# Three weight chunks ahead of the first gathers, and the rows of three experts turned by VectorE

## The chip, the cores and the metric

The kernel runs on one core of one Trainium2 chip. The metric is the device time of one execution in microseconds (us). TensorE does the matrix products, VectorE and ScalarE the element-wise work and the copies out of PSUM, GpSimd issues the gathers, scatters and accumulating DMAs, and SyncE issues the other DMAs.

## What is computed

Eight batches of eight heads go through a linear attention with a decay for each head, and the 4608 rows of 512 that come out go to eight experts. A routing by sorted scores gives each expert 576 rows.

```python
scores = scale * np.matmul(q, k.transpose(0, 1, 3, 2))
ret = scores * Dmat[None, :, :, :]          # gamma ** (i - j), lower triangle
x = np.matmul(ret, v)                        # -> 4608 x 512
...
for idx in order:                            # order = argsort(-(x @ w_gate).flatten())
    tok, e = idx // 8, idx % 8
    if assigned[tok] >= 0 or counts[e] >= 576: continue
    assigned[tok] = e; counts[e] += 1
...
for e in range(8):
    h = np.maximum(x[assigned == e] @ w1[e], 0.0)    # 512 -> 1024
    out[assigned == e] = h @ w2[e]                   # 1024 -> 512
```

## The kernel before

The attention runs over 16 units (a pair of batches by a pair of heads, loop `u`), its loads written ahead on SyncE's queue. Its rows go to a tile `xd` in DRAM. `Route` then finds the experts one after the other, in the order in which they fill up ("first" to "eighth" expert below, `e` = 0 to 7 in the code). For each it has a search in seven rounds (a matmul at L353, a chain of VectorE steps before and after), `members`, and `listing`, which writes the row numbers; what it does for the next experts is mixed into the products of the present one.

Each expert is a first layer `l1` and a second layer `l2`. `l1` works in 16 parts: eight blocks `f` of 128 features by two halves `s` of the tokens (256 and 320). A part is 12 matmuls, since weights and rows are each split into a high and a low half (`w1h`, `w1l`, `xh`, `xl`; three of four products are used). ScalarE writes the part's high half `hb` from PSUM (L1055), VectorE its low half (L1058). The parts' PSUM tiles have the tags `h0` and `h1` (by `s`), two buffers each, and `y` for the features 2 and 5. Parts alternate between the two halves; the first expert alone does the 256-token parts of `f` 0 to 3 first, then the 320-token ones. `l2` works in five groups `t` (four of 128 tokens, one of 64) of eight steps `f`, and each group's result `yt` is copied out (L1109; L1111 and a VectorE addition at L1112 for the last) and scattered by GpSimd (L1069).

A weight matrix comes in four chunks of 512 KB. `dma_pump` has SyncE fetch them into four `raw` buffers (L932) up to the limit `state['most']`; `conv` makes ScalarE write the high half (L946) and the negated low half (L951), to which GpSimd adds the chunk by an accumulating DMA (L952). With `fast`, VectorE makes the low half (L949). The limit is 2 until the first expert's rows are there: SyncE waits for the third gather (L1144), and after that the limit is 4, then open. `conv` is called in `l1` after the parts named in a list (L1063) and in `l2` at four steps.

The rows of an expert are gathered by GpSimd: five gathers of 128 rows (L983), then turned by TensorE (20 transposes at L1015, copied by ScalarE at L1017 and subtracted by VectorE at L1018). From `PIECES` on, 18 gathers of quarter rows (L971; VectorE makes their row numbers `quarter` at L476 to L480), turned by VectorE in blocks of 32 (L999), copied at L1001 and subtracted at L1002. All five blocks of such an expert are then written ahead of its first part.

The order in which all this is written is set by a planner (`Mixer`): it counts time for TensorE (`adv`: 320 or 400 for three matmuls of the first layer, 650 for a step of the second) and for VectorE (`vec`), and writes the next step of the search when its time has come. A gathered piece is due every 1300; the turning begins 6000 after the last piece (9000 after five whole gathers). Each engine then works through its own instructions in the order written. `warm` issues matmuls on constants, whose results nobody reads.

Of the kernel before, what the change touches and what calls it, by code (L numbers as in the profile page):

```python
# [19 lines left out]
NP, HP, NB = 4, 4, 9  # L20
N, DM, E, FF = 4608, 512, 8, 1024
SLACK = 1.0
PIECES = 6

def consts_np():
    h = np.arange(H); g = (1.0 - 2.0 ** (-5.0 - h)).astype(np.float64)
# [502 lines left out]
def attention(tc, nc, P, qk, vk, cst_d, wg_d, rf, xd, Lg, raw):  # L529
# [264 lines left out]
    def fills(u, g):  # L794
        for f, a in fill.get(2*u + g, []): f(*a)

    P['warm'](7)
    qscale(0, (0, 512))
    kscale(0, 0, 8)
    scores(0, 0)  # L800
# [92 lines left out]
def moe(tc, nc, P, R, xd, w1_d, w2_d, out, mix):  # L893
# [3 lines left out]
    ready = lambda k: len(found) > k  # L897
    regs, XG, quarters, parts = {}, {}, {}, {}
    xq = xd.rearrange("n (a c) -> (n a) c", a=4)
    state = dict(dma=0, conv=0, most=2, listing=-1)  # L900
    RAW, W1, W2, XH, XL = {}, {}, {}, {}, {}
    scat, lows = [], []
    spacer, spacer2 = [P['c'].tile([1, 1], F32, name=f"spacer{i}") for i in range(2)]
# [118 lines left out]
    def l1(e, tr):  # L1022

        hb = P['w'].tile([128, 8, 1152], F32R, name="hb", bufs=1)
        order = [(f, s) for f in range(8) for s in range(2)]
        if e == 0:
            order[:8] = [(f, s) for s in range(2) for f in range(4)]
        for i, (f, s) in enumerate(order):
            wh, wl = [w.rearrange("p (f d m) -> p f d m", f=2, d=4)[:, f % 2] for w in W1[e, f // 2]]
            if i == 0 and e >= PIECES:  # L1030
                for _ in tr:
                    pass
            if i == 0 and e:
                next(tr, None)
                next(tr, None)
            elif e == 0 and i in (2, 3):
                next(tr, None)
            elif i == (1 if e else 4):
                for _ in tr:
                    pass  # L1040
            xh, xl = XH[e], XL[e]
            c, n = ((slice(0, 256), 256), (slice(256, 576), 320))[s]

            ps = P['pp'].tile([128, n], F32, name="ph", tag="y" if f in (2, 5) else f"h{s}", bufs=2)
            terms = [(w[:, d], x[:, d, c]) for d in range(4) for w, x in ((wh, xh), (wh, xl), (wl, xh))]
            if e == 0 and f < 2:
                terms = terms[0::3] + terms[2::3] + terms[1::3]
            elif i in (2, 3) and e == 0:
                terms = terms[0::3] + terms[1::3] + terms[2::3]
            for k, (w, x) in enumerate(terms):  # L1050
                T.matmul(ps, w, x, start=(k == 0), stop=(k == 11))  # L1051
                if k % 3 == 2:
                    mix.adv(320 + 80*s, e == 0 and i < 3)
                    gather(e + 1)
            A.activation(hb[:, f, c], ps, AF.Relu)  # L1055
            for a, b in ((0, 256),) if s == 0 else ((0, 256), (256, 320)):
                to = (640 if a == 0 else 64) + 256*s
                V.scalar_tensor_tensor(hb[:, f, to+a:to+b], ps[:, a:b], 0.0, hb[:, f, 256*s+a:256*s+b].bitcast(F32),  # L1058
                                       op0=ALU.max, op1=ALU.subtract)
            mix.vec(340 + 140*s)  # L1060
            if e == 0 and i == 4:
                state['most'] = 8*E
            if i in ((2, 4, 7, 10) if e else (3, 5, 7, 9, 11, 13)):  # L1063
                conv()
        return hb

# [59 lines left out]
    def run():  # L1126
        mix.drain(lambda: 0 in regs)
        dma_pump()
        mix.drain(lambda: ready(0))
        conv(True)  # L1130
        conv()
        gather(0)
        lows.pop(0)()
        mix.step()
        warm(25)
        tr = transposes(0)
        next(tr)
        warm(4)
        next(tr)
        lows.pop(0)()  # L1140
        mix.step()
        warm(2)

        nc.sync.dma_start(spacer2, XG[0][0:1, 2, 0:1])  # L1144
        state['most'] = 4
        dma_pump()
        for e in range(E):
            tr = l2(e, l1(e, tr))
# [73 lines left out]
```

## Time and profile before

| what | value |
|---|---|
| three runs | 620.79, 623.42, 626.26 us; median 623.42 |
| profiled execution | 625.75 us, span 623.6 us |
| TensorE busy | 600.7 us (96%) |
| VectorE, ScalarE, GpSimd busy | 410.6, 271.6, 248.2 us |
| mean granted clock of TensorE | 0.988 of full speed |
| moved by DMA | 133.22 MB |

The span is the time from the first to the last instruction that the profile shows. The first expert's first layer begins near 168 us; the eighth expert ends near 620.

### The profile page before, as it was taken

What the parts mean: (1) busy time and instruction counts of PE and PEld (TensorE: products, weight loads), DVE (VectorE), ACT (ScalarE), POOL (GpSimd) and SP (SyncE); (2) the same over time, 40 slices, a digit from 0 to 9 for tenths busy, and PEclk for the clock granted to TensorE, in tenths of its full rate; (3) what the DMA queues carried; (4) which work ended last, traced back from release to release, by engine and by line L of the source; (5) the groups of instructions that cost most, each with busy time, mean ns of one, the idle gap of its engine ahead of it and who ended that gap; (6) DMA issues with size and microseconds to landing.
All of it is one profiled execution on the core that took longest, in us unless ns stands there. A gap on an engine that the chain in (4) does not pass through costs nothing.

```text
span 623.6 us, 14775 instructions
## 1 busy us (share of the span) xinstructions
PE 600.7 (96%) x5722; PEld 518.1 (83%) x5722; DVE 410.6 (66%) x1488; ACT 271.6 (44%) x465; POOL 248.2 (40%) x295
## 2 busy tenths in 40 slices
PE   7899999998989999999999999999999999999995
PEld 5788888875579779988987897799789889989983
DVE  4556788888868888887885877689478733322200
ACT  2244433333347355461652447155526445554410
POOL 4886665500302172061243242224313877832111
PEclk8899999999989999999999999999999999999998
DMA  9999899854768589787789399659937897994501
GB/s 330 408 369 401 280 370 316 261 140 137 192 180 194 174 221 264 186 207 236 156 224 246 94 229 227 201 111 231 247 114 174 200 245 169 259 249 124 102 35 42
DMA packets 53496, 133.22 MB, mean 214 GB/s; under 512 B 7410, under 2 KB 22642, under 8 KB 53426
## 3 DMA queue, kind: packets, MB, share of 16 engines
q0 software_dynamic: 15376, 51.92, 38.0%
q1 hardware_dynamic: 37906, 80.10, 38.0%
q8 instruction: 45, 0.74, 0.5%
q10 hardware_dynamic: 144, 0.26, 0.1%
q14 instruction: 25, 0.20, 0.1%
HBM read 80.35 MB, written 18.87 MB: 159 GB/s over the span
## 4 chain that ended last, share of the span: by engine, by line
PE 74%; DVE 9%; issue 6%; DMA 6%; POOL 2%; ACT 1%; SPq 1%; POOLq 0%; DVEq 0%
PE ph L1051 28%; PE py L1092 28%; PE sc L603 4%; PE px L647 3%; DMA xg<-xd,idx 2%; PE pS L624 2%; PE px L638 2%; PE pT L679 1%; DMA raw<-in_w 1%; PE r L353 1%; PE pt L1015 1%; DVE am L612 1%; DMA qin<-in_qk 1%; DVE cst L544 1%; DMA nin<-in_vk 1%
## 5 line engine op out<-in xcount | busy, mean ns | idle before, releaser
L1092 PE MATMUL py<-w2h,hb 128*128 128x512 f32 x576 | 187.3, 397 | 0.0
L1051 PE MATMUL ph<-xh,w1h 128*128 128x320 f32 (+1 forms) x512 | 151.7, 302 | 3.2 <-ACT xh L1017 3.2
L1051 PE MATMUL ph<-xh,w1l 128*128 128x320 f32 (+1 forms) x512 | 149.2, 297 | 0.0
L1051 PE MATMUL ph<-xl,w1h 128*128 128x320 f32 (+1 forms) x512 | 149.0, 297 | 0.0
L1092 PE MATMUL py<-w2l,hb 128*128 128x512 f32 (+1 forms) x320 | 125.3, 392 | 0.0
L1092 PEld LDWEIGHTS py<-w2h,hb 128*128 128x128 f32 x576 | 104.5, 188 | 21.7
L1051 PEld LDWEIGHTS ph<-xh,w1h 128*128 128x128 f32 x512 | 96.4, 191 | 4.4 <-ACT xh L1017 3.8
L1055 ACT ACTIVATE hb<-ph 128x256 fp32r<-128x256 f32 (+1 forms) x128 | 51.9, 408 | 105.1 <-PE ph L1051 96.3
L1051 PEld LDWEIGHTS ph<-xl,w1h 128*128 128x128 f32 x512 | 96.4, 191 | 0.3
L1051 PEld LDWEIGHTS ph<-xh,w1l 128*128 128x128 f32 x512 | 96.4, 191 | 0.0
L1058 DVE SCALAR_TENSOR_TENSOR hb<-ph,hb 128x256 fp32r<-128x256 f32 (+1 forms) x192 | 58.0, 352 | 46.2 <-ACT hb L1055 39.4
L1069 POOL DMA_INDIRECT out_y<-yt,idx x40 | 40.5, 1013 | 105.7 <-ACT yt L1109 70.5
L1092 PEld LDWEIGHTS py<-w2l,hb 128*128 128x128 f32 (+1 forms) x320 | 56.7, 177 | 12.9
L952 POOL DMA_DIRECT2D w2l<-raw x32 | 29.4, 919 | 87.2 <-ACT w2l L951 48.2
L612 DVE TENSOR_TENSOR am<-sc,cst 128x1024 f32<-128x1024 f32 x32 | 39.1, 1223 | 33.1 <-PE sc L603 33.0
L588 POOL TENSOR_TENSOR qin<-qin,cst 128x512 f32<-128x512 f32 (+1 forms) x48 | 48.3, 1034 | 31.2 <-DMA qin<-in_qk 27.3
L1109 ACT ACTIVATE yt<-py 128x512 f32<-128x512 f32 x32 | 19.2, 599 | 93.6 <-PE py L1092 70.0
L983 POOL DMA_INDIRECT xg<-xd,idx x30 | 30.2, 1008 | 71.9 <-DMA raw<-in_w 37.0
L627 ACT ACTIVATE st<-pS,cst 128x128 f32<-128x128 f32 x64 | 23.5, 368 | 79.9 <-PE pS L624 79.9
L952 POOL DMA_DIRECT2D w1l<-raw x31 | 29.0, 959 | 49.0 <-ACT w1l L951 32.5
L603 PE MATMUL sc<-qin,kin 64*128 64x128 f32 x512 | 38.8, 293 | 3.7 <-DVE am L612 1.9
L971 POOL DMA_INDIRECT xg<-xd,quarter x36 | 35.6, 989 | 12.8 <-issue 9.4
(191 smaller groups left out, 939.0 us busy)
## 6 DMA issues: line engine op xcount, KB each, us to landing
raw<-in_w SPq DMA_DIRECT2D x56, 512.0 KB
w2l<-raw POOLq DMA_DIRECT2D x32, 512.0 KB
w1l<-raw POOLq DMA_DIRECT2D x31, 512.0 KB
qin<-in_qk SPq DMA_DIRECT2D x14, 576.0 KB
kin<-in_qk SPq DMA_DIRECT2D x14, 576.0 KB
vin<-in_vk SPq DMA_DIRECT2D x14, 576.0 KB
nin<-in_vk SPq DMA_DIRECT2D x14, 512.0 KB
xd<-raw SPq DMA_DIRECT2D x36, 128.0 KB
```

The lines of the kernel that those rows point to most:

```text
L588: nc.gpsimd.tensor_tensor(x, x, e[:, None, :n].to_broadcast([128, (b-a)//n, n]), op=ALU.mult)
L603: nc.tensor.matmul(t[:, h, 128*j:128*j+128], blk(k, 4*g+j)[r], blk(q, 4*g+j)[r], start=(j == 0), stop=True, skip_group_check=True)
L612: nc.vector.tensor_tensor(a, SC[u, g].rearrange("p h (j q) -> p h j q", q=128), m1[:, u % HP, :, None, :].to_broadcast([128, 2, 4, 128]), ...
L627: nc.scalar.activation(s, p, AF.Copy, scale=ss[:, u % HP, c:c+1])
L952: add = lambda: nc.gpsimd.dma_start(lo, raw, accum_op=ALU.add)
L971: nc.gpsimd.indirect_dma_start(out=t[:, k, :], out_offset=None, in_=xq[:, :], in_offset=bass.IndirectOffsetOnAxis(ap=quarters[e][:, v:v+1] ...
L983: nc.gpsimd.indirect_dma_start(out=xg[:n, j, :], out_offset=None, in_=xd[:, :], in_offset=bass.IndirectOffsetOnAxis(ap=found[e][:n, j:j+1] ...
L1051: T.matmul(ps, w, x, start=(k == 0), stop=(k == 11))
L1055: A.activation(hb[:, f, c], ps, AF.Relu)
L1058: V.scalar_tensor_tensor(hb[:, f, to+a:to+b], ps[:, a:b], 0.0, hb[:, f, 256*s+a:256*s+b].bitcast(F32), op0=ALU.max, op1=ALU.subtract)
L1069: st = nc.gpsimd.indirect_dma_start(out=out[:, :], out_offset=bass.IndirectOffsetOnAxis(ap=found[e][:n, t:t+1], axis=0), in_=y[:n], in_off ...
L1092: T.matmul(ps[:m], a, w, start=(k == 0), stop=(k == last), skip_group_check=True)
```

## The change

The limit of chunks before the gathers is 3 instead of 2; the third chunk's conversion stands behind the first two blocks' transposes, ahead of the first expert's loop, and is taken out of the loop's list. `PIECES` is 5 instead of 6: the sixth expert joins the seventh and the eighth in having its rows gathered by quarters and turned by VectorE (its weights are then read in the layout `w1n`). For these three, the 256-token parts of `f` 0 to 3 come first, as they do for the first expert, and of their five blocks at most three are written ahead of the first part, one each ahead of the third and the fourth, the rest ahead of the fifth. At the start of the attention 12 matmuls of `warm` instead of 7.

```diff
-PIECES = 6
+PIECES = 5
...
-    P['warm'](7)
+    P['warm'](12)
...
-    state = dict(dma=0, conv=0, most=2, listing=-1)
+    state = dict(dma=0, conv=0, most=3, listing=-1)
...
-        if e == 0:
+        if e == 0 or e >= PIECES:
             order[:8] = [(f, s) for s in range(2) for f in range(4)]
...
-            if i == 0 and e >= PIECES:
-                for _ in tr:
-                    pass
             if i == 0 and e:
+                for _ in range(3 if e >= PIECES else 2):
+                    next(tr, None)
+            elif (e == 0 or e >= PIECES) and i in (2, 3):
                 next(tr, None)
-                next(tr, None)
-            elif e == 0 and i in (2, 3):
-                next(tr, None)
-            elif i == (1 if e else 4):
+            elif i == (4 if e == 0 or e >= PIECES else 1):
                 for _ in tr:
                     pass
...
-            if i in ((2, 4, 7, 10) if e else (3, 5, 7, 9, 11, 13)):
+            if i in ((2, 4, 7, 10) if e else (5, 7, 9, 11, 13)):
                 conv()
...
         next(tr)
         lows.pop(0)()
+        conv()
         mix.step()
```

## Rows read from the trace of the kernel before

**Rows 1.** Busy time by stretches: stretch, then each engine's us, clock, DMA share, GB/s.

```profile
404.10:460.70 56.60, 56.60 (x402) 49.70 (x401) 42.04 (x181) 26.72 (x42) 17.47 (x23) 1.00 0.75 192
460.70:513.90 53.20, 53.20 (x338) 47.71 (x338) 35.92 (x138) 26.88 (x42) 30.90 (x36) 1.00 0.75 181
```

**Rows 2.** Timeline of TensorE: start, us, instruction, idle time before it and its releaser.

```profile
17.51 0.45 PE L624 MATMUL pS<-vin,ks 128*64 128x64 f32 x8 [2.07 <-POOL ks L593]
...
179.00 1.44 PE L1051 MATMUL ph<-xh,w1h 128*128 128x320 f32 x4 [3.02 <-ACT xh L1017]
```

**Rows 3.** Busy time by stretches, behind these two idle times.

```profile
18.60:21.90 3.30, 3.30 (x44) 2.85 (x42) 0.00 (x0) 0.96 (x2) 3.30 (x4) 0.50 1.03 413
...
179.00:182.35 3.35, 3.35 (x12) 3.35 (x13) 0.41 (x1) 0.00 (x0) 0.97 (x1) 0.50 1.00 302
```

**Rows 4.** Timeline of ScalarE around the first expert's first layer.

```profile
169.99 0.38 ACT L1055 ACTIVATE hb<-ph 128x256 fp32r<-128x256 f32 x1 [1.79 <-issue]
...
176.68 1.06 ACT L946 ACTIVATE w1h<-raw 128x1024 fp32r<-128x1024 f32 x1 [0.70 <-DMA raw<-in_w]
...
178.58 0.36 ACT L1017 ACTIVATE xh<-pt 128x256 fp32r<-128x256 f32 x1
```

**Rows 5.** Timeline of SyncE's queue, the first expert's weight chunks.

```profile
157.08 0.89 SPq L932 DMA_DIRECT2D raw<-in_w  x2
...
172.25 13.30 SPq L932 DMA_DIRECT2D raw<-in_w  x5
```

**Rows 6.** Busy time of a stretch of the attention with idle time.

```profile
73.40:78.00 4.60, 3.59 (x73) 3.19 (x73) 4.46 (x8) 1.67 (x5) 2.31 (x3) 1.00 0.53 117
```

**Rows 7.** The same for the stretch behind the second chunk's landing.

```profile
162.50:163.50 1.00, 1.00 (x6) 0.45 (x5) 1.00 (x3) 1.00 (x2) 0.70 (x2) 1.00 0.00 0
```

**Rows 8.** Timeline of TensorE at the start.

```profile
1.48 3.17 PE L1175 MATMUL warm<-full 128*128 128x512 bf16 x7 [1.48 <-DVE full L1161]
6.37 0.83 PE L603 MATMUL sc<-qin,kin 64*128 64x128 f32 x10 [1.72 <-POOL qin L588]
```

**Rows 9.** Timeline of TensorE, first and last of the sixth expert's five runs of transposes.

```profile
431.75 0.51 PE L1015 MATMUL pt<-ident,xg 128*128 128x128 f32 x4
432.09 0.70 PE L1092 MATMUL py<-w2h,hb 128*128 128x512 f32 x2
...
436.12 0.51 PE L1015 MATMUL pt<-ident,xg 64*128 64x64 f32 x4
436.55 0.74 PE L1092 MATMUL py<-w2h,hb 128*128 128x512 f32 x2
```

**Rows 10.** Busy time of VectorE alone while it makes `quarter`.

```profile
477.85:479.38 1.53, 1.35 (x9) 1.00 0.56 102
```

**Rows 11.** Timeline of GpSimd: first gathers of the first, sixth, seventh expert, the seventh's last.

```profile
162.03 1.15 POOL L983 DMA_INDIRECT xg<-xd,idx  x1 [37.01 <-DMA raw<-in_w]
...
422.62 1.07 POOL L983 DMA_INDIRECT xg<-xd,idx  x1 [1.73 <-DVE room L494]
...
479.66 1.07 POOL L971 DMA_INDIRECT xg<-xd,quarter  x1 [2.21 <-DVE eb L504]
...
508.39 0.96 POOL L971 DMA_INDIRECT xg<-xd,quarter  x1 [0.30 <-issue]
```

**Rows 12.** Timeline of VectorE, turning the seventh expert's rows.

```profile
506.70 0.71 DVE L999 STREAM_TRANSPOSE xz<-xg 128x512 f32<-128x512 f32 x1
507.34 0.65 DVE L1002 TENSOR_TENSOR xl<-xz,xh 128x512 fp32r<-128x512 f32 x1
...
513.07 0.45 DVE L999 STREAM_TRANSPOSE xz<-xg 128x256 f32<-128x256 f32 x1 [2.79 <-DMA xg<-xd,quarter]
...
514.64 0.68 DVE L1112 TENSOR_TENSOR yt<-yt,py 64x512 f32<-64x512 f32 x1 [0.22 <-ACT yt L1111]
```

**Rows 13.** The chain that ended last, a piece of a second layer.

```profile
328.63 5.56 PE py L1092 x24
```

**Rows 14.** Busy time of VectorE alone in one round of the search.

```profile
455.88:458.70 2.82, 2.50 (x13) 1.00 0.51 173
```

## The prediction

> **What bounds the kernel now.** I read the busy time by stretches first. In the sixth expert's 53.2 us, as in the fifth's 56.6, TensorE is busy for every microsecond, VectorE for two thirds or more, GpSimd for a third to over a half [rows 1]. So a microsecond is won in three ways only: less work on TensorE, less idle time of it, or a higher granted clock. Then I listed TensorE's idle times. One stands out in the expert stage: 3.02 us in the first expert, ended by ScalarE's copy into `xh` at L1017 [rows 2]. The stretch behind it is granted 0.50, 1.2 in place of 2.4 GHz [rows 3]. ScalarE's own order tells why the copy is late: it stands behind the two conversions of a weight chunk (L946, L951), which begin at 176.68 when the chunk lands, and ends at 178.94 [rows 4]. SyncE issued that chunk at 172.25, as it has to wait for the gathered rows first (L1144); the two chunks before it went out at 157.08 [rows 5].
>
> **First expert: third chunk early, its conversion before the loop.** The transposes of the last block end at 175.98, 3.02 before 179.00 [rows 2]. With the conversions gone, the copy (0.36) [rows 4] follows at once, and the part of 320 tokens begins near 176.5: idle time 0.5 in place of 3.0, a gain of 2.5. That part has 12 matmuls in 3.35 us at 0.50 [rows 3]; at full clock they take half, so 1.65 more, if the clock stays. The stretch around 73.4 to 78, with 1.0 us idle, kept 1.00 [rows 6]; 2.1 us (15.4 to 17.5) and 3.02 us were followed by 0.50 [rows 2, 3]. I count 1.65 in full. Sum: -4.15.
> Where the conversion goes: ScalarE stands idle for 1.79 us up to 169.99 [rows 4], and the conversions need 2.1 (two of 1.06). The first activation of the loop starts some 0.3 later; its bank is wanted again three parts on, so that is nothing. If the chunk were not there by then, ScalarE would wait in front of the copies, as now, and the gain would be gone; but two chunks issued at 157.08 are in at 162.0 [rows 11], and no byte moves from 162.5 to 163.5, ahead of the first gather's rows [rows 7]. 512 KB at 413 GB/s, the rate when the engines are full [rows 3], is 1.3 us. So the third chunk fits between 162 and 163.5 almost whole. I charge 0.2 for its tail; its bounds are 0 and 1.3 (all of it ahead of the gathers), and a fall of the clock on top.
> On GpSimd the accumulating DMA is the next thing behind the five gathers, before as after, only earlier; on SyncE the third issue (0.45) is followed only by the wait at L1144. The chunk for features 768 on is now alone behind that wait. Cost nothing; should it come late, there are ten parts until it is used.
> **The 12 warm-up matmuls.** Five more at the pace of the seven (0.45) are 2.3 us, against 1.72 idle before the first scores [rows 8]: at most 0.5 late, less if the clock is up by then. What follows waits for the loads and GpSimd's scaling until 17.5 [rows 2], whatever TensorE does before it. Taken as 0, bounds -0.5 and +0.5.
> **Sixth expert: TensorE's transposes go.** Five runs of four, each between two `py` matmuls; by start to start the first costs 0.34, the last 0.43, the five 1.63 together [rows 9]. Gain 1.6.
> What replaces it: 18 gathers instead of 5 on GpSimd. They start 1.5 us later (eight small VectorE steps for `quarter`, L476 to L480, 1.53 in all) [rows 10], at 424.1 instead of 422.6, and the run of 18 with the weight and output DMAs among them took 479.66 to 508.39 for the seventh expert [rows 11]: the last starts near 453 to 454 and is in memory 4.7 us later (508.39 to 513.07) [rows 11, 12], at 458.5. The expert's first layer starts at 460.7 - 1.6 = 459.1. The weight accumulations queued among the gathers come some 5 us later, and they are wanted 10 us or more after that: nothing.
> When is it turned? I counted the planner's own figures (a piece each 1300, turning 6000 after the last piece, a step of the second layer 650). For the kernel before they put the seventh expert's first turn at step f=4 of group t=3, ahead of `yt`'s addition, as the trace has it [rows 12]. For the change they put the sixth expert's turns at t=3, f=5 to t=4, f=2, directly behind the search round after f=3, with the next round ahead of the last block.
> VectorE's queue then is, from the end of the second layer (459.1) backwards: the last group 3.7, four steps of 0.70 (24 matmuls in 5.56) [rows 13], so that round's matmul is done at 452.5. A round holds VectorE for 2.8 (455.88 to 458.70) [rows 14]: free at 455.3. Seven turns and subtractions at 0.65 [rows 12] take it to 459.9; the second block's low half, the fifth of them, is ready at 458.6, in time for the first part. The next round, 2.8, to 462.7. Last block 0.45, ScalarE's copy 0.4, its `yt` copy 0.6, VectorE's addition 0.7, and the first part's low half 0.4: 465.2. This is the new wait: with four 256-token parts in a row, the fourth takes the PSUM bank of the first (tag h0, two buffers, the third part uses y). Parts of 256 take 256/320 of 1.7, 1.4, so the fourth is due at 459.1 + 4.2 + a search matmul 0.2 = 463.6. TensorE waits 1.5. In the order before, that bank was wanted three parts later. Whether the clock falls behind 1.5 us lies between the rows (1.0 kept it, 2.1 did not): 0 or up to 1.65, taken as 0.
> **Seventh expert.** The turns put into the search by the planner (1310 a block in place of 610) push its listing from the ninth part of the first layer to the eleventh, 3200 by the same count, or 3.4 us (a part of 1280 takes 1.4): the gathers start that much later against the first layer's start. Before, the last block was there 0.9 before that start (513.07 against 513.9); now it comes 2.5 behind it. From there the same chain, 0.45 + 0.45 + 0.6 + 0.7 + 0.4 = 2.6, gives 5.1, and the bank is due at 4.3: a wait of 0.8. In the old order it would have been 2 or more, since the second part wants all blocks.
> **Eighth expert.** Its rows are there far ahead; the order alone costs nothing.
> **Sum.** -4.15 + 0.2 - 1.6 + 1.5 + 0.8 = -3.25. The profiled execution (625.75, span 623.6) would become 622.5; the median of the three runs, 623.42, becomes 620.2.
>
> **Rivals.** *No new waits.* If VectorE runs as far ahead as it did for the seventh expert before (its third block turned at 506.7, 7 us ahead of need) [rows 12], the waits of 1.5 and 0.8 vanish: -5.55, 617.9. For it: TensorE idles nowhere in the last three experts. Against: there the search was over, while in the fifth expert's stretch, where the sixth's rows are turned, VectorE has 42 of 56.6 us of work [rows 1].
> *The turning comes too late (slower).* Place: end of the sixth expert's second layer. If the seventh's pieces are written later than I count, by three steps of 650, the turns fall into the first layer and stand behind `yt`'s addition: 0.6 + 0.7, then five operations of 0.65 until the second block's low half, 4.6 us of idle TensorE, and 1.65 for the clock. -3.25 - 0.8 + 6.25 = +2.2: 625.6. It decides from those three steps on; my count leaves just this much, and it met the order before. The same at the sixth expert as well would come to 630.
> *The third chunk holds up the first gathers.* In the trace before, the gathers' rows do not move before 163.5 [rows 7], and GpSimd's first gather starts at 162.03, released by that chunk's landing as the trace puts it [rows 11]. If that is no accident, the third chunk's 1.3 us is paid in full, TensorE's warm-up runs out, and the clock may fall: 1.1 to 2.75 worse than the forecast, 621.3 to 623.0; the change then gives little. Here a rule of the Trainium skill speaks against the change: "DMA: Bandwidth & Descriptors", section "SWDGE vs HWDGE vs iDMA", has GpSimd's and SyncE's transfers in different queues of the same engines, served in turn. By that rule gathers beside a chunk get a part of the engines' time instead of waiting behind it, so a cost between nothing and this rival's; no run so far shows a chunk beside the first gathers.
> *It does not do what it says:* the chunk lands after 168.2, and ScalarE waits in front of the loop: no gain of 4.15, 624.3.
>
> **How the numbers follow.** Forecast 0.45, no new waits 0.25, late turning 0.10, held gathers 0.17, no effect 0.03. The range takes the forecast with waits of 0 to 3 in place of 2.3, and the first three rivals: the low end, 616.5, is the first rival less the start's 0.5 and less 0.9, since the three runs of before lie 5.5 us apart; the high end is the second. A measurement of this kernel tells 1% from nothing, 6.2 us: under 617.2 is reached only by the first rival with a little help at the start (0.18), over 629.7 only by late turning twice (0.06).
>
> **What would show it.** After: no idle over 1 us before L1051 in the first expert, clock 1.00 there, conversions of the third chunk in front of the first activation; the first gather at 162.0 to 162.4; no L1015 in the sixth expert; idle time before the fourth first-layer part of the sixth and seventh experts, released by L1058 or L1055. I am wrong if the first gather starts over 1 us later, if the clock falls in the sixth expert, or if `yt`'s addition stands ahead of the seventh's turns.

## The result, and the profile after

| | before | after |
|---|---|---|
| median (22 runs each, side by side) | 622.37 us (619.87 to 626.26) | 628.02 us (622.13 to 632.8) |
| ratio of after to before, 95% interval | | 1.0061 (1.0041 to 1.0080) |
| profiled execution, span | 625.75, 623.6 us | 631.76, 630.0 us |

By the ratio the change makes the kernel slower by 0.6%, 3.8 us; the forecast was 3.2 us faster, and 628.0 lies outside its range. Executions that were slow as a whole (four of after's 22, from 631.60 us up, the profiled one among them) are left out of every ratio and of the medians under "The experiments"; after's median without them is 627.0. The profiled execution of after lies 3.7 us over its own median, so what its trace shows is read stage by stage, and the sizes are taken from the repeated runs.

A table by stage is made from TensorE's timeline: the start of the first matmul of each layer, and the difference to the next one's start. Only these stages differ by more than 0.1 us:

| stage | before | after | difference | forecast |
|---|---|---|---|---|
| attention, up to the first expert's first layer | 168.25 | 171.48 | +3.23 | 0 |
| first expert, first layer | 33.78 | 30.95 | -2.83 | -3.95 |
| third expert, second layer | 30.16 | 29.79 | -0.37 | 0 |
| fifth expert, second layer | 29.71 | 27.56 | -2.15 | -1.6 |
| sixth expert, first layer | 26.84 | 28.38 | +1.54 | +1.5 |
| seventh expert, first layer | 25.59 | 32.05 | +6.46 | +0.8 |
| eighth expert, second layer, to the end | 33.19 | 33.68 | +0.49 | 0 |

They sum to 6.4, the difference of the two spans. One row carries the result: the seventh expert. It stands in other profiles too: turn_only and chunk_turn below, with the same turning, have 30.41 and 29.63 us there, 4.8 and 4.0 over before. The timeline of TensorE in the kernel after (start, duration, instruction, and in brackets the idle time before it and what ended it) has these idle times over 0.45 us, of the ones that matter here. Line numbers are those of each run's own kernel; L1048 here is L1051 of the kernel before.

```profile
18.25 0.45 PE L624 MATMUL pS<-vin,ks 128*64 128x64 f32 x8 [2.87 <-POOL ks L593]
...
37.73 0.49 PE L603 MATMUL sc<-qin,kin 64*128 64x128 f32 x4 [1.83 <-DVE am L612]
...
179.56 0.85 PE L1048 MATMUL ph<-xh,w1h 128*128 128x320 f32 x4 [0.47 <-ACT xh L1017]
...
182.08 0.85 PE L1048 MATMUL ph<-xl,w1h 128*128 128x320 f32 x4 [1.08 <-DVE xl L1018]
...
464.49 0.39 PE L1048 MATMUL ph<-xh,w1h 128*128 128x256 f32 x1 [1.26 <-DVE hb L1055]
...
521.11 0.58 PE L1048 MATMUL ph<-xh,w1h 128*128 128x256 f32 x1 [3.46 <-DVE hb L1055]
```

The busy time by stretches of the kernel after (stretch; us in it, then busy us of TensorE, its weight loads, VectorE, ScalarE, GpSimd; granted clock, DMA share, GB/s) says what the clock did behind these waits:

```profile
18.70:22.10 3.40, 3.40 (x44) 2.95 (x42) 0.00 (x0) 1.25 (x3) 3.38 (x5) 0.50 1.02 410
39.20:42.60 3.40, 3.40 (x48) 3.28 (x50) 1.30 (x2) 1.08 (x3) 1.09 (x3) 0.50 1.02 345
179.00:182.40 3.40, 1.84 (x12) 1.49 (x11) 2.79 (x11) 0.46 (x2) 0.00 (x0) 1.00 0.97 336
...
521.10:527.30 6.20, 6.19 (x25) 6.19 (x26) 1.04 (x3) 2.16 (x4) 4.98 (x6) 0.50 0.24 56
```

In the first expert the 3.02 us of idle time [rows 2] is now 0.47, and the stretch behind it, at 0.50 before [rows 3], runs at 1.00. That is the gain of the third chunk. But a new wait of 1.08 stands two steps behind, for the low half of the last block. VectorE's timeline of the kernel after shows what holds it:

```profile
177.51 0.69 DVE L1018 TENSOR_TENSOR xl<-pt,xh 128x512 fp32r<-128x512 f32 x1
178.12 0.14 DVE L357 SCALAR_TENSOR_TENSOR cs<-room,r 32x8 f32<-32x8 f32 x1
...
181.05 0.19 DVE L348 TENSOR_TENSOR u<-v,D 128x36 f32<-128x36 bf16 x1
181.27 0.42 DVE L1055 SCALAR_TENSOR_TENSOR hb<-ph,hb 128x256 fp32r<-128x256 f32 x1
181.61 0.41 DVE L1018 TENSOR_TENSOR xl<-pt,xh 128x256 fp32r<-128x256 f32 x1
```

From L357 at 178.12 to the end of L348 at 181.24 is one round of the search, 3.1 us against the 2.8 of [rows 14], and the last block's `xl` is queued behind it. In the kernel before, TensorE's wait for `xh` hid that.

In the seventh expert the 3.46 us are ended by VectorE's `hb`, as forecast for 0.8, and the stretch of 6.2 us behind it is granted 0.50, which costs about half of that. The same timeline a little earlier, VectorE first and GpSimd under it, to be held against [rows 11, 12]:

```profile
517.18 0.71 DVE L999 STREAM_TRANSPOSE xz<-xg 128x512 f32<-128x512 f32 x1 [4.28 <-DMA xg<-xd,quarter]
...
518.50 0.45 DVE L999 STREAM_TRANSPOSE xz<-xg 128x256 f32<-128x256 f32 x1
...
520.04 0.68 DVE L1109 TENSOR_TENSOR yt<-yt,py 64x512 f32<-64x512 f32 x1 [0.19 <-ACT yt L1108]
520.65 1.07 DVE L1055 SCALAR_TENSOR_TENSOR hb<-ph,hb 128x256 fp32r<-128x256 f32 x3
```

```profile
482.67 1.08 POOL L971 DMA_INDIRECT xg<-xd,quarter  x1 [5.77 <-DVE eb L504]
...
507.77 0.96 POOL L971 DMA_INDIRECT xg<-xd,quarter  x1 [0.30 <-issue]
508.74 1.00 POOL L952 DMA_DIRECT2D w1l<-raw  x1
510.04 1.06 POOL L971 DMA_INDIRECT xg<-xd,quarter  x1 [0.30 <-DMA xg<-xd,quarter]
511.39 1.04 POOL L971 DMA_INDIRECT xg<-xd,quarter  x1 [0.30 <-issue]
512.74 1.00 POOL L971 DMA_INDIRECT xg<-xd,quarter  x1 [0.30 <-issue]
```

Two things are late. The first of the 18 pieces is issued 30.5 us ahead of the layer's start (482.67 to 513.20) where it was 34.1 (479.66 to 513.77), so 3.6 later; 3.4 was forecast. And the 16th piece, issued at 510.04, lets VectorE go on only at 517.18, 7.1 later, where the last piece before took 4.7 [rows 11, 12]. Between the 15th and the 16th stands the accumulating DMA of a weight chunk (508.74); in the kernel before, the one at that place came behind the 18th (508.39 in [rows 11]), as GpSimd's timeline there has it:

```profile
509.35 1.02 POOL L952 DMA_DIRECT2D w1l<-raw  x1
```

### The profile page after: what moved, and what is told of

It reads as the page before. It is cut to its first block, busy times and chain, and to the rows that moved or that the text cites. A ratio compares the mean times of both kernels' runs of the same rounds, so it can differ in the third digit from the quotient of the medians.

```text
span 630.0 us, 14771 instructions
## 1 busy us (share of the span) xinstructions
PE 601.3 (95%) x5703; PEld 518.6 (82%) x5707; DVE 416.3 (66%) x1501; ACT 271.7 (43%) x465; POOL 263.5 (42%) x308
## 4 chain that ended last, share of the span: by engine, by line
PE 72%; DVE 9%; DMA 7%; issue 7%; POOL 3%; ACT 1%; SPq 1%; POOLq 0%; DVEq 0%
PE ph L1048 31%; PE py L1089 25%; PE sc L603 3%; PE px L647 2%; PE px L638 2%; PE r L353 2%; PE pS L624 2%; DVE am L612 1%; DMA xd<-raw 1%; PE pt L1015 1%; DMA w1l<-raw 1%; PE pT L679 1%; DMA xg<-xd,quarter 1%; DVE cst L544 1%; DMA nin<-in_vk 1%
## 5 line engine op out<-in xcount | busy, mean ns | idle before, releaser
L1048 PE MATMUL ph<-xh,w1h 128*128 128x256 f32 (+1 forms) x512 | 152.7, 304 | 5.4 <-DVE hb L1055 4.7
L1048 PE MATMUL ph<-xl,w1h 128*128 128x256 f32 (+1 forms) x512 | 149.8, 298 | 1.1 <-DVE xl L1018 1.1
L1048 PE MATMUL ph<-xh,w1l 128*128 128x256 f32 (+1 forms) x512 | 149.9, 298 | 0.0
L1048 PEld LDWEIGHTS ph<-xh,w1h 128*128 128x128 f32 x512 | 97.1, 192 | 7.0 <-DVE hb L1055 5.1
L1048 PEld LDWEIGHTS ph<-xl,w1h 128*128 128x128 f32 x512 | 97.2, 192 | 1.6 <-DVE xl L1018 1.3
L1048 PEld LDWEIGHTS ph<-xh,w1l 128*128 128x128 f32 x512 | 97.0, 192 | 0.0
L971 POOL DMA_INDIRECT xg<-xd,quarter x54 | 54.8, 1014 | 25.1 <-issue 14.3
L983 POOL DMA_INDIRECT xg<-xd,idx x25 | 25.3, 1013 | 72.3 <-DMA raw<-in_w 40.3
L593 POOL TENSOR_TENSOR ks<-nin,cst 128x512 f32<-128x512 f32 x32 | 32.8, 1045 | 22.7 <-issue 21.3
```

What stands on the lines that cost most here:

```text
L593: nc.gpsimd.tensor_tensor(KS[u][:, a:b], LD[u, 'n'].rearrange("p (a d) -> p a d", d=64)[:, a:b], ks[:, u % HP, a:b, None].to_broadcast([12 ...
L971: nc.gpsimd.indirect_dma_start(out=t[:, k, :], out_offset=None, in_=xq[:, :], in_offset=bass.IndirectOffsetOnAxis(ap=quarters[e][:, v:v+1] ...
L983: nc.gpsimd.indirect_dma_start(out=xg[:n, j, :], out_offset=None, in_=xd[:, :], in_offset=bass.IndirectOffsetOnAxis(ap=found[e][:n, j:j+1] ...
```

## The experiments

The change has three parts that can be made alone: the third chunk, the turning on VectorE with its order of parts, and the warm-up. All runs below are five rounds beside the kernel before on the same chip; its medians there were 622.75 to 622.97. A ratio of 0.001 is 0.62 us.

| kernel | median us | ratio to before, 95% interval |
|---|---|---|
| chunk_only | 620.72 | 0.9966 (0.9943 to 0.9988) |
| warm_only | 624.52 | 1.0028 (0.9999 to 1.0058) |
| turn_only | 625.03 | 1.0029 (1.0005 to 1.0054) |
| chunk_turn | 624.06 | 1.0026 (0.9995 to 1.0058) |
| order_only | 623.89 | 1.0006 (0.9976 to 1.0036) |
| turn_lean | 629.74 | 1.0107 (1.0061 to 1.0152) |
| chunk_hold | 618.89 | 0.9934 (0.9900 to 0.9968) |
| warm_gap | 623.25 | 1.0007 (0.9972 to 1.0041) |
| turn_queue | 626.16 | 1.0040 (1.0002 to 1.0077) |
| turn_first | 628.35 | 1.0089 (1.0053 to 1.0125) |
| turn_again | 631.35 | 1.0132 (1.0108 to 1.0156) |
| queue_again | 626.68 | 1.0064 (1.0042 to 1.0086) |
| mended | 622.25 | 0.9978 (0.9952 to 1.0004) |
| after_mended | 623.73 | 1.0010 (0.9986 to 1.0034) |

The first four ran on one chip, the next four on a second, turn_queue and turn_first on a third, the last four on the second again.

**The parts of the change alone.** chunk_only is the kernel before with

```diff
-    state = dict(dma=0, conv=0, most=2, listing=-1)
+    state = dict(dma=0, conv=0, most=3, listing=-1)
...
-            if i in ((2, 4, 7, 10) if e else (3, 5, 7, 9, 11, 13)):
+            if i in ((2, 4, 7, 10) if e else (5, 7, 9, 11, 13)):
...
         lows.pop(0)()
+        conv()
```

> The kernel before with the third chunk alone. My theory: the idle 3.02 us and the half clock behind it go, of which the profile after gave back 2.8 us in the first expert's first layer: 2 to 3.5 us faster than before (ratio 0.995 to 0.997), the start of that layer unchanged. Rival, the chunk holds up the gathers or pushes other transfers: that layer starts 1 us or more later and the time is within 1 us of before.

It is 2.1 us faster (0.7 to 3.6). Its TensorE timeline has the same two waits as after:

```profile
173.63 0.85 PE L1051 MATMUL ph<-xh,w1h 128*128 128x320 f32 x4 [0.47 <-ACT xh L1017]
...
176.16 0.85 PE L1051 MATMUL ph<-xl,w1h 128*128 128x320 f32 x4 [1.10 <-DVE xl L1018]
```

So the gain is real and smaller than its term of 3.95, and the wait behind the search round belongs to this part.

warm_only changes one number:

```diff
-    P['warm'](7)
+    P['warm'](12)
```

> The kernel before with 12 warm-up matmuls in place of 7. The profile after had the first expert's first layer 3.2 us later than the profile before, all of it from the attention. My theory: that is chance of one profiled execution, so the time is within 1 us of before and that layer starts at 168 to 169 us. Rival, the longer warm-up shifts the clock's fall at the start and delays the attention: 2 to 3.5 us slower (ratio 1.003 to 1.006), the layer starts near 171.5.

1.7 us slower, with an interval that just reaches nothing; yet its profile has the first expert start at 164.50, earlier than any other profile here. turn_only is the rest of the diff (`PIECES = 5`, the order of the parts and the steps of `tr` in `l1`):

```diff
-PIECES = 6
+PIECES = 5
...
-        if e == 0:
+        if e == 0 or e >= PIECES:
             order[:8] = [(f, s) for s in range(2) for f in range(4)]
```

> The kernel before with the sixth expert's rows turned by VectorE and the new order of parts, without the third chunk and with 7 warm-up matmuls. My theory: the second layer of the fifth expert loses 2 us, the sixth expert's first layer gains 1.5, the seventh's gains 3 to 6.5 (idle time behind late quarter rows and the half clock after it): 3 to 6 us slower than before, and the whole of the loss of the change is here. Rival, the loss is from the attention: within 1.5 us of before.

It is 1.8 us slower on this chip: the fifth's second layer 2.15 shorter, the sixth's first 1.54 longer, the seventh's first 30.41 in place of 25.59, with a wait of 3.03 and a clock fall. From the first expert's start on its profile is 4.2 us longer than that of before, more than its runs say: one profile is not the median. chunk_turn has both:

> The changed kernel with 7 warm-up matmuls in place of 12. If the parts add up and the warm-up is nothing, it stands to before as the changed kernel does (ratio 1.006, 3.8 us slower). If the warm-up cost the attention's 3.2 us, it is within 1 us of before.

At 1.0026 it is not told apart from turn_only, and it takes no more than a part of after's loss; the sum of the three parts is +1.4 us against after's 3.8, which the intervals allow.

**Is it the order of the parts, or the late rows?** order_only is the kernel before with the new order in the seventh and eighth experts alone, where rows are turned on VectorE in any case:

```diff
-        if e == 0:
+        if e == 0 or e >= PIECES:
             order[:8] = [(f, s) for s in range(2) for f in range(4)]
...
-            elif i == (1 if e else 4):
+            elif i == (4 if e == 0 or e >= PIECES else 1):
```

> The kernel before, with one thing changed: in the first layers of the seventh and eighth experts the four 256-token parts stand behind the four 320-token parts, as in the change. The sixth expert stays as it was, so no rounds move onto VectorE and the seventh's token rows aren't listed later. Theory (the new order is harmless as long as the rows come in time; the harm of the change is the late rows): within 1.5 us of the kernel before, 621.5 to 624.5, no wait over 1.0 us of TensorE in the seventh expert's first parts and the clock at 1.00 there. Rival (the order alone makes the fourth 256-token part wait for a PSUM bank that the turning still holds): 1.5 to 2.5 us slower, with a wait of 1.2 us or more ahead of that part in both experts.

(In the run, as in the change, the four 256-token parts stand ahead of the 320-token ones, not behind them.)

The time is that of before, and the seventh's first layer shows no idle time at all by stretches:

```profile
509.54:535.12 25.58, 25.58 (x193) 25.58 (x192) 7.97 (x23) 13.85 (x24) 18.03 (x19) 1.00 0.88 208
```

So the order costs nothing when the rows are there: they are what is late. turn_lean leaves the planner's charge for the sixth expert's turning at the old figure, to have the seventh listed earlier:

```diff
-                mix.vec(700)
+                mix.vec(700 if e > PIECES else 610)
...
-                    mix.vec(610)
+                    mix.vec(610 if e > PIECES else 0)
```

> The turning half of the change alone (rows of the sixth expert turned on VectorE, parts reordered in the last three experts), but with the charge for the sixth expert's turning in the planner left at what it was for TensorE's, so that the seventh expert's rows should be listed about two parts earlier than in the run with the turning half alone. Theory (the seventh expert's wait is late rows, through the planner's charge): its pieces come some 3 us earlier, the wait of 3.0 us falls to under 0.8, the clock stays at 1.00 there, and the sum is -2.2 for the sixth expert's transposes, +1.5 for its wait, 0 to +0.8 for the seventh's: 0.1 to -0.7 against the kernel before, and 2 to 3 us under the run with the turning half alone. Rival (the wait comes from VectorE's work in the parts themselves, whenever the rows land): the wait stays at 2.5 us or more, with the clock fall, and the time stays at +1 to +2.5.

The first piece came 34.5 us ahead of the layer's start (483.18 to 517.66), as in the kernel before, and the seventh's wait was gone. But the time did not fall: 1.0107 here, 1.0132 for turn_again below, which is turn_only on this chip, and the intervals overlap. The list of TensorE's waits from 427 to 535 us (what waited, for whom: total, times, longest):

```profile
PE r L353 <- DVE G L177: 4.5, 2, 2.5
PE ph L1048 <- DVE hb L1055: 3.6, 2, 3.5
```

From 476 on there is none. The loss moved from the seventh expert to the sixth: in the sixth's first layer a search matmul (L353) stands in TensorE's queue 1.99 us before VectorE has made its `G`, and the fourth part waits 3.48 where it waited 1.26. That layer takes 34.47 us, 28.41 in turn_again; the seventh's takes 25.59, 29.63 there. The other search matmul, 2.53 in the fifth's second layer, is not this edit's alone: turn_again waits 1.23 and 1.39 for the same there. So a smaller charge gains nothing.

**The first expert's search round.** chunk_hold is chunk_only and one number more:

```diff
-                    mix.adv(320 + 80*s, e == 0 and i < 3)
+                    mix.adv(320 + 80*s, e == 0 and i < 4)
```

> The chunk half of the change alone (third chunk ahead of the gathers, warm-up at 7), and the search round of VectorE that stood ahead of the last block's low half held back by one part more in the first expert. Theory (the 1.1 us wait ahead of the fourth 256-token part is that round): the wait goes to under 0.3, the first expert's first layer takes 30.0 us rather than 31.1, and the time is 1.0 to 1.5 under that of the run with the chunk half alone (ratio to the kernel before 0.994 to 0.995). Rival (something else is as late: the ScalarE half, or the search comes back as a wait for the second expert's list): a wait of 0.8 or more stays there or turns up ahead of the second expert's rows, and the time is within 0.5 of the chunk half alone.

The theory holds. TensorE's timeline has the 0.47 alone, VectorE's has the low half ahead of the round, the layer takes 29.94 in place of 31.10, and the ratio is 0.9934:

```profile
176.43 0.70 PE L1051 MATMUL ph<-xh,w1h 128*128 128x320 f32 x3 [0.47 <-ACT xh L1017]
```

```profile
176.41 0.42 DVE L1018 TENSOR_TENSOR xl<-pt,xh 128x256 fp32r<-128x256 f32 x1
177.41 0.15 DVE L357 SCALAR_TENSOR_TENSOR cs<-room,r 32x8 f32<-32x8 f32 x1 [0.57 <-PE r L353]
```

This is the fastest kernel of the study: 4.1 us (2.0 to 6.2) under the kernel before. Some of it lies further on, where the moved round shifts what follows: the second expert's second layer takes 29.78 in place of 30.59, the third's first 27.78 in place of 27.24. By the ratios it is 2.0 us under chunk_only, on different chips, where 1.0 to 1.5 was expected.

**The idle time in the attention.** warm_gap puts eight constant matmuls in the kernel before where TensorE waits for GpSimd near 15 to 17 us:

```diff
+                if u == 0 and g:
+                    P['warm_t'](8)
```

> The kernel before with 8 matmuls on constants put where TensorE waits for GpSimd's scaling near 17.5 us (2.1 to 2.9 us idle in the profiles so far). Theory (the clock fall that follows that wait stands on the path of the attention): the rows show 1.00 over 18 to 22 us, and the first expert starts 1 to 1.5 us earlier than in the kernel before; the time is 0.5 to 1.5 us lower. Rival (the wait's end is not moved, and the clock there is hidden by GpSimd's or VectorE's own pace): the clock stays at 1.00 but the first expert's start moves by less than 0.5 us, and the time is within 0.5 us of the kernel before. A third outcome: the matmuls themselves end late and cost up to 1.7 us.

By stretches the clock stayed up, where it was 0.50 before [rows 3], and the time is not told apart from that of before:

```profile
18.50:21.90 3.40, 3.40 (x69) 3.02 (x68) 0.00 (x0) 1.33 (x3) 3.40 (x5) 1.00 1.02 412
```

This does not decide. The interval, 1.7 us lower to 2.6 higher, holds the theory's 0.5 to 1.5 as well as the rival's nothing, and in this profile the first expert starts at 166.62, 1.6 earlier than in that of before, which is the theory's sign. So it is not shown that the fall is off the path, and all 16 profiles side by side speak against it. The granted clock from 16 to 164 us is 1.00 in ten of them, where the first expert starts at 164.5 to 167.2 (turn_again: 169.0); 0.99 in before, chunk_turn, chunk_hold and after_mended, with 167.9 to 168.5; 0.98 in after and mended, with 171.5 and 172.1. The +3.23 of the first table goes with this: after has two stretches at 0.50 there (18.7 and 39.2, above), before has one. A stretch of 3.4 us at 0.50 costs 1.7 by itself, an estimate from half the clock, and the start moves by some 3; whether the fall makes the delay or comes with it, no run separates. The wait alone does not: warm_only has the same idle time, 2.84 us up to 17.35, a clock of 1.00 behind it, and the earliest start.

**The gather queue.** turn_queue is turn_only with one DMA moved: the accumulation of the seventh's fourth weight chunk is issued when the last piece has been.

```diff
-            if ready(0) and 0 not in XG:
+            if hold:
+                held.append(add)
+            elif ready(0) and 0 not in XG:
...
                 gather(e + 1)
+                if held and e + 1 in XG:
+                    held.pop()()
...
-                    conv()
+                    conv(hold=want == 1 and e + 1 == 6 and e + 1 not in XG)
```

> The turning half of the change alone, with one transfer moved: GpSimd's accumulating DMA of the seventh expert's fourth weight chunk (w1l<-raw), which in the run with the turning half alone was issued between the 15th and the 16th piece of the seventh's rows, is issued after the 18th. ScalarE's conversions stay where they are. Theory (the 16th piece took 7 us from its issue because it stood behind that accumulation in the software queue, where 4.7 us were seen in the kernel before): the last two blocks are turned about 2 us earlier, the seventh's wait falls from 3.0 to 0.6 to 1.2 us, the clock stays at 1.00 behind it, the seventh's first layer takes 26.5 to 27.0 us instead of 30.4, and the time is 3 to 3.5 us below that of the turning half alone: -0.5 to -1 of the kernel before. Rival (the late listing alone makes the wait; pieces take what they take): the block still starts 6.5 us or more behind the 16th piece's issue, the wait stays at 2.5 to 3.0 with the clock fall, and the ratio stays at 1.003.

The seventh's wait vanished and its first layer took 25.72; but the time was 1.0040, since the fifth's second layer took 31.93, not 27.56. turn_first also moves a search round behind the sixth's last block:

```diff
-                mix.adv(650)
+                mix.adv(650, e == 4 and e + 1 in XH)
...
-                    mix.adv(320 + 80*s, e == 0 and i < 3)
+                    mix.adv(320 + 80*s, e == 0 and i < 3 or e == 5 and i < 2)
```

> As the run before it (the accumulation moved), and the search round of VectorE (2.6 us) that stood ahead of the last block of the sixth expert's rows is placed behind it and behind the first two parts' low halves. Theory (the sixth expert's wait of 1.26 us is that round): the wait goes to under 0.3 and the sixth's first layer takes 27.0 us, not 28.4; the round comes some 3 us later, so the seventh's rows are listed 2 to 4 us later, and its wait comes back at 2 to 4 us with the clock fall: in sum within 1.5 us of the run before it, because VectorE has one stretch of slack and both experts want it. Rival (the list isn't behind that round, or there is room after it): both waits under 1 us and the time 1 to 1.5 us below the run before it, 2 us below the kernel before.

GpSimd's and TensorE's timelines:

```profile
485.10 1.07 POOL L975 DMA_INDIRECT xg<-xd,quarter  x1 [3.57 <-DVE eb L504]
```

```profile
471.28 0.38 PE L1052 MATMUL ph<-xh,w1h 128*128 128x320 f32 x1 [1.48 <-DVE hb L1059]
...
519.72 0.39 PE L1052 MATMUL ph<-xh,w1h 128*128 128x256 f32 x1 [2.01 <-DVE hb L1059]
```

The theory's trade came, and worse: the sixth's wait only moved to a later part (the layer took 28.87), the first piece was issued 28.2 us ahead of the seventh's start instead of 30.5, and the seventh's wait was back. It is 3 us slower than turn_queue, with an interval that just reaches nothing.

**The two side by side.** turn_again and queue_again are turn_only and turn_queue unchanged, now on one chip.

> The turning half of the change alone, once more, beside the run with the accumulation moved. Theory (the late signals that lengthened the fifth expert's second layer belong to the conditions of a run): that layer takes 31 to 32 us here too, the seventh's first layer 29 to 31, and the time is 3 to 5 us over the kernel beside it. Rival (they belong to the program): the layer takes 27.6, the seventh's 30.4, and the time is within 1.5 us of the kernel beside it.

> The turning half with the accumulation of the seventh's fourth weight chunk issued behind the last piece. Theory: seventh's wait under 0.6 us and its first layer 25.6 to 26.0, as before; the fifth's second layer as in the kernel beside it; ratio to the kernel before 0.997 to 1.004. Rival: the fifth's second layer at 31.9 while the kernel beside it has 27.6.

The accumulation is worth 4.2 us (1.0132 against 1.0064; about 2 to 6). The timeline of turn_again, GpSimd, VectorE and TensorE, then of queue_again:

```profile
511.69 1.01 POOL L952 DMA_DIRECT2D w1l<-raw  x1
513.00 1.06 POOL L971 DMA_INDIRECT xg<-xd,quarter  x1 [0.30 <-issue]
...
518.82 0.71 DVE L999 STREAM_TRANSPOSE xz<-xg 128x512 f32<-128x512 f32 x1 [3.09 <-issue]
...
522.75 0.39 PE L1048 MATMUL ph<-xh,w1h 128*128 128x256 f32 x1 [2.27 <-DVE hb L1055]
```

```profile
512.23 0.94 POOL L975 DMA_INDIRECT xg<-xd,quarter  x1 [0.30 <-issue]
513.18 1.00 POOL L954 DMA_DIRECT2D w1l<-raw  x1
...
515.59 0.45 DVE L1003 STREAM_TRANSPOSE xz<-xg 128x256 f32<-128x256 f32 x1 [0.74 <-DMA xg<-xd,quarter]
...
518.47 0.38 PE L1052 MATMUL ph<-xh,w1h 128*128 128x256 f32 x1 [0.18 <-DVE hb L1059]
```

With the accumulation in front, the 16th piece (513.00) is turned 5.8 us after its issue; without it the 18th (512.23) 3.4 after. The 16th itself, without the accumulation, is seen in after_mended below, which has the same edit: issued at 508.68, turned 4.1 later, at 512.79.

```profile
512.79 0.71 DVE L1003 STREAM_TRANSPOSE xz<-xg 128x512 f32<-128x512 f32 x1 [0.45 <-DMA xg<-xd,quarter]
```

TensorE's wait ahead of the fourth part is 2.27 in the first, 0.18 in the second.

The other half of what was expected came in part: the fifth's second layer takes 30.48 and 30.51 in these two, less than the 31 to 32 expected but 2.9 over turn_only's 27.56. So its lengthening isn't made by the moved DMA, and it does not belong to the program alone. The timeline of TensorE and VectorE around the search in turn_only, then in turn_again, the same program:

```profile
433.61 0.39 PE L353 MATMUL r<-oh,G 128*128 128x32 bf16 x9
434.04 0.15 DVE L357 SCALAR_TENSOR_TENSOR cs<-room,r 32x8 f32<-32x8 f32 x1 [0.85 <-PE r L353]
```

```profile
437.93 0.39 PE L353 MATMUL r<-oh,G 128*128 128x32 bf16 x9 [1.23 <-DVE G L177]
441.50 0.15 DVE L357 SCALAR_TENSOR_TENSOR cs<-room,r 32x8 f32<-32x8 f32 x1 [3.51 <-remote]
444.58 0.39 PE L353 MATMUL r<-oh,G 128*128 128x32 bf16 x9 [1.39 <-DVE G L177]
```

VectorE takes up the search's matmul 0.43 us after its start in the one, 3.57 after in the other, and TensorE, which runs on meanwhile, then stands before the next one. The trace names `remote` as what VectorE waited for, not the matmul; which signal that is, and why it came late, is not shown.

**Both waits cured.** mended is the whole change with the edits of chunk_hold and turn_queue and the warm-up at 7; after_mended has it at 12, and is thus the change with those two edits.

> The whole change with the warm-up at 7, the first expert's search round held back one part more, and the seventh's accumulation behind the last piece. If the two waits are what the change lost, the time is that of the chunk half with the round held (0.9934) plus that of queue_again beside it: 2 to 4 us under queue_again, ratio 0.991 to 0.998. If the halves disturb each other, it stays within 1 us of queue_again.

> As mended, with the warm-up at 12, that is the whole change with both cures. If the longer warm-up costs what the run with it alone said (1.7 us, with an interval from 0 to 3.6), it is 1 to 2.5 us over mended; if that was chance, within 1 us of it. Against the changed kernel (1.0061 of the kernel before) it should be 4 to 6 us faster.

mended is 4.4 us under queue_again beside it by the medians, 5.4 by the ratios, a little more than expected: within the noise the halves add up. after_mended is 1.0010 where the change itself was 1.0061, so the two cures take back some 3 us of its 3.8 (on different chips), less than the 4 to 6 expected. Its profile shows both waits gone: the first expert's first layer takes 29.47, the seventh's 25.69. (mended's, at 630.97 us far over its median, has 27.86 in the seventh.) But the fifth's second layer takes 32.08, where before has 29.71 and after 27.56: here TensorE waits 0.55 and 2.03 us ahead of search matmuls, the clock falls behind the second (0.50 from 440.4 to 443.8), and the gain from the missing transposes has become a loss of 2.4. Neither edit touches that. after_mended is 2.0 us over mended by the ratios, the third comparison in a row in which the longer warm-up is the slower one (the others are warm_only at +1.7 and after against chunk_turn at +2.2, the last on different chips); each of the three intervals by itself still reaches zero. Neither version beats chunk_hold.

## Why the prediction was wrong, point by point

- **Seventh expert, +0.8: the step that failed.** Its mechanism was right: the rows come late, the turning stands behind them, the fourth 256-token part waits for its bank, released by `hb`. Also right were the 3.4 us by which the listing moves (3.6). Wrong was "now it comes 2.5 behind it": I moved the 18 gathers as a block and kept 4.7 us from issue to memory. The move shifted them past an accumulation in the same software queue. That accumulation took 1.3 us of GpSimd's order ahead of the 16th piece (508.74 to 510.04), and the piece then took 7.1; its block was turned 4.0 behind the layer's start, the last block 5.3 behind it (518.50 to 513.20). By the forecast's own chain of 2.6 that is 7.9 against a bank due at 4.3, 3.6 us of wait, and 3.46 was measured. With the accumulation behind the pieces the last block stands 1.8 behind the start (515.59 to 513.83), and by the forecast's own chain of 2.6 that is 4.4 against a bank due at 4.3: the 0.18 us of wait that queue_again shows. The Trainium skill says, in "DMA: Bandwidth & Descriptors", section "Two DMAs through the same engine are not ordered", that descriptors of one queue of one engine start in order; the landings agree with that, 5.8 to 7.1 us behind an accumulation and 3.4 to 4.1 without. The prediction did ask what the gathers do to the accumulations, for the sixth expert, and not what the accumulations do to the gathers.
- **The clock behind the waits, "taken as 0".** With a wait of 3.46 in place of 0.8 it fell, 6.2 us at 0.50, and nearly doubled the loss: 3.46 + 3.0 = 6.46. In turn_only it was 3.03 + 1.8, in chunk_turn 2.53 + 1.5. For the sixth's 1.26 and the first's 1.08 it stayed at 1.00, as taken.
- **First expert, -3.95.** The idle time of 2.5 and the clock's 1.65 came as worked out (3.02 to 0.47; 1.00 in that stretch), and a new wait of 1.1 took part of it. The prediction said what VectorE had to do in the sixth and seventh experts, instruction by instruction, and not here: it costed ScalarE's half of the block and left out the low half. chunk_hold shows that wait to be the round: held back, it is gone. About 0.2 of the difference in this layer (4.15 - 1.08 against 2.83) is not placed. And the 1.65 is not won in every execution: of the ten profiles without the third chunk, all with an idle time of 2.2 to 3.0 us at this place, eight show the fall behind it; in warm_gap and turn_lean (2.38 and 2.27 us) the clock stayed at 1.00, and the layer took 31.44 and 31.81, against 33.78 in before and 31.10 in chunk_only. The 2.1 us that chunk_only's runs gain lie between these.
- **Sixth expert.** -1.6 for the transposes was -2.15; the forecast took the starts of the transposes to the starts behind them, and left out that the pair of matmuls behind a run takes 0.70 to 0.74 [rows 9], where a pair without a run ahead of it takes 0.62 in the same timeline: five times 0.1 more. +1.5 for the wait came as 1.54 in the layer, of which TensorE's wait is 1.26. The queue of VectorE worked out there held in its order, and the bank came free 6.1 us behind the layer's start, as forecast (465.2 to 459.1; 464.49 to 458.43).
- **Warm-up, 0 with bounds of 0.5.** Three comparisons put it at +1.7 to +2.2. Its cause isn't settled: no profile shows a stage that is longer by that much with it every time. The start of the first expert moves between 164.5 and 172.1 us over the profiles of all kernels, with the clock falls in the attention, and of the three profiles with 12 matmuls one has no such fall, one has one and one has two. The +3.23 of the profile after is of that kind and was not counted as the change's.
- **The eighth expert.** The order alone costs nothing, as forecast (33.16 to the end in order_only). But its second layer to the end takes 33.66 to 33.68 in all ten profiles with `PIECES` at 5 and 33.16 to 33.19 in the other six: 0.5 us for which the prediction has no term. TensorE's last matmul ends 25.65 us behind the layer's start in before and in turn_only alike, so it lies behind the products; what makes it was not tried.
- **The rivals.** The third chunk does not hold up the gathers: the first starts 6.26 us ahead of the first matmul (165.22 to 171.48), before 6.22 (162.03 to 168.25). That it came 3.2 later in itself, one of the prediction's signs of being wrong, is the whole attention's delay in that profile; in chunk_only it starts at 159.28, 6.14 ahead of the first matmul. The slower rival named the seventh expert and the clock, with the price 6.25, near the 5.66 by which that term was missed; but it had the turns behind `yt`'s addition, and they stayed ahead of it (518.50, 520.04).

In sum: -2.1 from the chunk, +1.8 (0.3 to 3.4) from the turning on one chip and +8.2 (6.7 to 9.7) on another, about +1.7 from the warm-up; the change as a whole +3.8.

## What to carry to other kernels

When a run of transfers moves, write down what is queued between and ahead of them at the new place, on the same queue; the price of a piece is its row only for the neighbours that it had there. When the last wait of a stage is cured, work out the next operand of the same instructions as well: here the high half was early and the low half stood behind a round of the search. And work moved from a full engine to one that is two thirds busy need not be a gain if a chain of short dependent steps lives there: VectorE had the microseconds, but not between the search's rounds.

## What the runs showed of the hardware that was not expected

- The same program took 625.03 us on one chip and 631.35 on another, while the kernel before had 622.96 and 622.75 there. Of these 6 us the fifth expert's second layer has 2.9 by the two profiles; the rest is not placed. There VectorE takes up the search's matmul 3.57 us after its start in place of 0.43 (the rows above), and in one round of this layer it is 3.6 to 4.8 us in all seven profiles on the second and the third chip that have the sixth expert's rows turned by VectorE. order_only on the second chip, without that turning, has 0.43 there:

```profile
441.67 0.39 PE L353 MATMUL r<-oh,G 128*128 128x32 bf16 x9
442.10 0.15 DVE L357 SCALAR_TENSOR_TENSOR cs<-room,r 32x8 f32<-32x8 f32 x1 [3.99 <-PE r L353]
```

  So neither the chip nor the turning makes it alone. The Trainium skill, in "Perfetto Trace Analysis", section "Per-engine timelines", says that a matmul's end in a trace is an estimate and that its semaphore follows only when PSUM has acknowledged the data, so lateness of that kind can't be seen on TensorE's own rows; no run here shows that it is of that kind.
- The length of an idle time alone does not say whether the clock falls. At one place in the program, ahead of the first expert's first part of 320 tokens, the clock stayed at 1.00 behind 2.38 us in warm_gap and was 0.51 behind 2.34 us in order_only, by the stretches of the two:

```profile
176.50:179.90 3.40, 3.37 (x30) 3.27 (x31) 1.32 (x6) 0.44 (x1) 0.99 (x1) 1.00 0.93 254
175.20:178.50 3.30, 3.30 (x12) 3.30 (x13) 0.59 (x2) 0.00 (x0) 0.97 (x1) 0.51 0.97 318
```

  Elsewhere it was 0.50 behind 1.83 us (39.2 to 42.6 in after) and 1.00 behind 2.01 in turn_first, by the stretch

```profile
519.80:523.50 3.70, 3.70 (x28) 3.70 (x29) 0.95 (x3) 1.99 (x4) 2.79 (x4) 1.00 0.71 220
```

so the prediction's interpolation between 1.0 and 2.1 was no rule.
